# QK-norm attention with a max-out feed-forward layer: two-transfer row loads, fewer turning products, alternating spread products, idle products at the start, and first-layer bounds by one ones-product

## The chip, the core and the metric

The kernel runs on one core of a Trainium2 chip. The metric is the device time of one execution in microseconds (us), from the first instruction to the last with the little that lies around it. The time before is the median of three runs. One further execution was recorded by the hardware profiler; every duration below is from that execution.

The core has five engines, each with its own instruction stream that it works through in order: TensorE (PE in the profile; its weight loads are PEld) multiplies matrices into PSUM; VectorE (DVE), ScalarE (ACT) and GpSimd (POOL) work on elements; SyncE (SP) issues most of the DMA transfers, and ACT's stream issues some.

## The reference

```
def rmsnorm(x, g):
    rms = np.sqrt(np.mean(x * x, axis=-1, keepdims=True) + 1e-06)
    return x / rms * g
q_n, k_n = (rmsnorm(q, g_q), rmsnorm(k, g_k))
scores = np.matmul(q_n, k_n.transpose(0, 1, 3, 2)) / np.sqrt(64)
scores = scores - np.max(scores, axis=-1, keepdims=True)
attn = np.exp(scores)
attn = attn / (np.sum(attn, axis=-1, keepdims=True) + 1e-09)
x = np.matmul(attn, v)          # then heads side by side: 3584 x 768
h = np.maximum(np.maximum(x @ w1, x @ w2), x @ w3)
return (h @ w_out).astype(np.float32)
```

q, k and v are 8 batches of 12 heads of 448 tokens of 64 values; each of the four weight matrices is 768 x 768; everything is float32.

## The kernel before

Two heads make a pair; there are 48 pairs, g = 0 to 47. A pair's 896 rows of q (or k) lie as seven blocks of 128 rows: even blocks and the lower half of the last one hold the first head, odd blocks and its upper half the second. Of each pair, squares, row sums, an inverse root and a scaling normalise q and k (squares, sum_squares, inv_rms, scale_rows); the result is turned so that the 64 values lie across partitions; scores, softmax, and the product with v follow. A score tile is 128 queries of both heads against 448 keys; a pair has three such tiles and a fourth of 64 queries each.

The first six pairs (PLAIN = 6) work in plain float32: their rows are turned by TensorE (turn_whole writes the tile rows, keep_whole copies it to kt and qt), the exponentials are turned by TensorE (turn_plain, keep_turned), and the sums are inverted (inverse_sums), spread over the partitions by products with the identity (spread_sums) and applied at the end (scale_plain). Later pairs split every operand in two float16 parts and are turned by DMA.

The feed-forward layer multiplies with weights split in two float16 parts. load_raw brings a block of raw weights, prep_block decodes it (one step on ACT, three on DVE), and after three blocks of one row of output features bound_in finds a bound of that row's columns: 18 products of the block with itself (tile marks), the largest entry of each row on DVE, then the largest over the partitions, which the helper largest does by a turning product, a DVE reduction over one partition and a product with a row of ones. From the bound come a root on POOL, a copy, a reciprocal and a multiply on DVE (w_most, w_up), and the two-part split of the three blocks (upper on ACT, lower on DVE).

The order is written out by hand. Every engine runs its instructions in the order in which the program makes them. The main loop goes through 12 beats for each pair (beat(g, i)); in a beat stand pieces of pair g (softmax, scores), of g - 1 (values), of g + 1 (turning) and of g + 2 (squares), plus units of the feed-forward layer (thirds) from the seventh pair on. later(n, work) puts work n beats behind the present one; bound_in and prep_block use it, and one weight block is taken every four beats, so that six rows of features are prepared in six pairs and a little more.

Ahead of the loop stands the opening: loads of pairs 0 and 1 and of the first three raw blocks, normalisation of both pairs, the product of the two gains (the tile gain; column and gain_c carry it to partitions; prep_gain derives factors for later pairs), turning of pair 0, and the first score tile.

A ring of three PSUM buffers (tag "m") serves marks, rows, spread and the small tiles; score tiles have two buffers of their own.

## Time and profile before

| what | us |
|---|---|
| median of three runs (1033.67, 1035.94, 1036.47) | 1035.94 |
| the profiled execution, time | 1033.57 |
| its span, first to last instruction | 1031.8 |
| mean granted TensorE clock | 0.985 |
| TensorE busy, 0 to 10 us | 0.82 |
| TensorE busy, 300 to 400 us | 100.00 |

The table is read from its ends. The profile's busy times say how full an engine was, not whether it set the time: TensorE is 96% busy over the whole span, but nearly idle at first, full from 300 us on, and in between it shares the work with VectorE, which is fuller than TensorE in some stretches. A change in an early stretch has to be read from that stretch.

### The profile page before, as it was taken

How to read it: one execution, taken by the hardware profiler on the slowest of the kernel's cores; microseconds unless marked ns; L12 is line 12 of the kernel's file. 1: busy time of each engine (PE TensorE's matmuls, PEld its weight loads, DVE VectorE, ACT ScalarE, POOL GpSimd, SP SyncE). 2: the span in 40 equal slices, each digit the busy share in tenths (PEclk: the TensorE clock that was granted, in tenths of full speed). 3: DMA queues.
4: the chain of work that ended last, by engine and by line, in shares of the span. 5: the costliest groups of instructions: out<-in, count | busy, mean ns of one | idle time of the engine just before them, and what ended most of it. 6: DMA issues, size and time to landing. Idle time of an engine off the chain costs nothing.

```text
span 1031.8 us, 17413 instructions
## 1 busy us (share of the span) xinstructions
PE 988.9 (96%) x5988; PEld 530.6 (51%) x5988; DVE 697.5 (68%) x1343; ACT 622.8 (60%) x1419; POOL 598.5 (58%) x652
## 2 busy tenths in 40 slices
PE   5999789898899999999999999999999999999998
PEld 3655444444455555555555555555555555555555
DVE  4898989987676856776667767786777666760120
ACT  3787866667666676666665666666665766651111
POOL 5566676765766666756666576676675766410000
PEclk9999879999999999999999999999999999999999
DMA  8866698997999999999999899999999998861001
GB/s 200 202 178 172 165 204 164 177 166 134 209 173 171 167 182 210 168 172 151 221 171 188 152 216 181 177 169 180 193 168 169 179 201 145 135 104 59 1 1 62
DMA packets 524089, 165.99 MB, mean 161 GB/s; under 512 B 500321, under 2 KB 519777, under 8 KB 524001
## 3 DMA queue, kind: packets, MB, share of 16 engines
q1 hardware_dynamic: 460992, 148.89, 74.8%
q10 hardware_dynamic: 63008, 16.00, 8.7%
q8 instruction: 47, 0.77, 0.3%
q14 instruction: 42, 0.34, 0.1%
HBM read 53.35 MB, written 11.01 MB: 62 GB/s over the span
## 4 chain that ended last, share of the span: by engine, by line
PE 74%; DVE 2%; ACT 1%; DMA 1%; issue 1%; SPq 0%; ACTq 0%
PE acc L841 41%; PE acc L903 15%; PE av L812 8%; PE sc L633 8%; PE sc L640 1%; DVE pp L767 1%; DVE nm L655 1%; DMA pt<-pp 1%; ACT sc L671 0%; DVE w_sb L335 0%; DVE ss L413 0%; DMA out_dram<-osb 0%; SPq L786 0%; ACT w_sb L330 0%; ACT pp L757 0%
## 5 line engine op out<-in xcount | busy, mean ns | idle before, releaser
L841 PE MATMUL acc<-xt,w_sb 128*128 128x448 f16 x2592 | 516.8, 355 | 0.0
L841 PEld LDWEIGHTS <-w_sb 128*128 128x128 f16 x2592 | 252.5, 98 | 245.0 <-issue 16.8
L671 ACT ACTIVATE sc<-sc,nm 128x448 f32<-128x448 f32 x294 | 178.8, 608 | 197.0 <-DVE nm L655 192.5
L655 DVE TENSOR_REDUCE nm<-sc 128x2 f32<-128x896 f32 x192 | 186.3, 970 | 101.5 <-PE sc L640 51.4
L757 ACT ACTIVATE pp<-sc,rs 128x448 f16<-128x448 f32 x294 | 172.8, 633 | 77.9 <-issue 29.2
L767 DVE SCALAR_TENSOR_TENSOR pp<-sc,rs,pp 128x448 f16<-128x448 f32 x294 | 188.0, 675 | 3.3 <-ACT pp L757 3.2
L427 POOL TENSOR_TENSOR ri<-ri,half_neg 128x7 f32<-128x7 f32 x96 | 148.8, 1550 | 8.0
L903 PE MATMUL acc<-w_sb,ht 128*128 128x384 f16 x864 | 148.6, 327 | 0.0
L461 POOL TENSOR_TENSOR kp<-kn,kp 128x448 f16<-128x448 f32 x42 | 44.7, 1065 | 167.6 <-ACT kp L455 154.5
L633 PE MATMUL sc<-kt,qt 128*128 128x448 f16 x504 | 117.6, 356 | 10.4 <-DVE pp L767 7.7
L903 PEld LDWEIGHTS <-ht 128*128 128x128 f16 x864 | 83.8, 99 | 60.2 <-issue 5.8
L633 PEld LDWEIGHTS <-qt 128*128 128x128 f16 x504 | 48.8, 98 | 56.0 <-issue 6.9
L812 PE MATMUL av<-pt,vp 128*64 128x448 f16 x672 | 72.2, 355 | 0.7 <-DMA pt<-pp 0.6
L870 POOL COPY hx<-ht 128x128 f16<-128x128 f16 x48 | 15.3, 318 | 94.3 <-DVE ht L865 94.3
L413 DVE TENSOR_REDUCE ss<-sq 128x7 f32<-128x448 f32 x96 | 57.6, 601 | 11.4 <-ACT sq L404 8.3
L595 POOL TENSOR_TENSOR vp<-vr,vp 128x512 f16<-128x512 f32 x42 | 50.0, 1189 | 22.6 <-ACT vp L589 22.6
L750 DVE TENSOR_SCALAR rs<-sc 128x2 f32<-128x2 f32 (+1 forms) x168 | 26.2, 156 | 50.4 <-ACT sc L671 50.3
L827 DVE SCALAR_TENSOR_TENSOR xt<-av,xt 128x448 f16<-128x448 f32 x42 | 26.2, 623 | 49.0 <-ACT xt L826 49.0
L461 POOL TENSOR_TENSOR qp<-qn,qp 128x448 f16<-128x448 f32 x42 | 46.2, 1100 | 19.2 <-ACT qp L455 16.9
L855 DVE TENSOR_TENSOR m<-acc,m 128x448 f32<-128x448 f32 x48 | 29.6, 617 | 37.7 <-PE acc L841 37.5
L812 PEld LDWEIGHTS <-vp 128*64 128x64 f16 x672 | 35.0, 109 | 35.0 <-issue 15.5
L861 ACT ACTIVATE ht<-acc 128x448 f16<-128x448 f32 x48 | 26.2, 546 | 41.8 <-DVE acc L855 41.8
(130 smaller groups left out, 1181.4 us busy)
## 6 DMA issues: line engine op xcount, KB each, us to landing
raw<-in_moe_w_dram SPq DMA_DIRECT2D x18, 768.0 KB, 4.5
kt<-kt SPq DMA_DIRECT2D x84, 112.0 KB, 2.5
out_dram<-osb SPq DMA_DIRECT2D x24, 384.0 KB, 3.7
vr<-in_v_dram SPq DMA_DIRECT2D x42, 192.0 KB, 4.1
kr<-in_k_dram ACTq DMA_DIRECT2D x34, 224.0 KB, 3.3
qr<-in_q_dram ACTq DMA_DIRECT2D x34, 224.0 KB, 4.6
raw<-in_moe_w_out_dram SPq DMA_DIRECT2D x6, 768.0 KB, 5.0
vs<-vp SPq DMA_DIRECT2D x84, 48.0 KB, 2.1
```

Source lines behind the costliest of these rows:

```text
L413: nc.vector.tensor_reduce(sums[g % 2][:, KQ[what]], sq, axis=AX, op=ALU.add)
L427: nc.gpsimd.tensor_tensor(out=ri, in0=ri, in1=half_neg[:, at], op=ALU.pow)
L461: nc.gpsimd.tensor_tensor(out=parts[:, :, 1], in0=n, in1=parts[:, :, 0], op=ALU.subtract)
L595: nc.gpsimd.tensor_tensor(out=vp[:, 1], in0=values_of(g).rearrange("p h n d -> p (h n) d"), in1=vp[:, 0], op=ALU.subtract,)
L633: nc.tensor.matmul(sc[:, h, :S], qt[:, 4 * h + c], kt[:, n, keys[h]], start=n == 0, stop=n == 1,)
L655: nc.vector.tensor_reduce(nm[:, :n], sc[:, :n, :S], axis=AX, op=ALU.max, negate=True)
L671: nc.scalar.activation(to, sc[:, h, :S], AF.Exp, bias=nm[:, h:h + 1], accum_out=total,)
L757: nc.scalar.activation(pp[:, h, 0], sc[:, h, :S], AF.Copy, scale=rs[:, h:h + 1])
L767: nc.vector.scalar_tensor_tensor(out=pp[:, h, 1], in0=sc[:, h, :S], scalar=rs[:, h:h + 1], in1=pp[:, h, 0], op0=ALU.mult, op1=ALU.subtract,)
L812: nc.tensor.matmul(av[half, :S], values, pt[:, 7 * h + block, SHIFT[h]:SHIFT[h] + S], start=n == 0, stop=n == len(steps) - 1,)
L841: nc.tensor.matmul(acc[:, :S], wt[:, wp, c], xs[c][:, xp], start=(c == 0 and n == 0), stop=(c == NCT - 1 and n == 2),)
L903: nc.tensor.matmul(acc[:, :HW], lhs, wo_sb[:, f, wp, half * HW:(half + 1) * HW], start=(f == 0 and n == 0), stop=(f == NFT - 1 and n == 2),)
```

## The change

Seven edits, all in work that is done ahead of the later part of the span.

1. Row loads of the first six pairs take two transfers (four blocks and three blocks) in place of three. For pair 0 the second transfer of q goes to ACT's queue.
2. load_v brings the first batch's v in three transfers of four consecutive rows a partition, in place of four transfers of single rows; keep_whole writes kt in the matching order of keys.
3. turn_whole turns the last block by two 64 x 64 products on separate quarters of the array, in place of three products; kt and qt are 448 columns wide, in place of 512.
4. spread_sums goes through the column halves in alternation.
5. 36 products of the identity with itself, read as bfloat16, stand at the start of TensorE's stream; their result is not used.
6. In the opening the squares of pair 1 stand behind those of pair 0, the sums and roots of pair 1 move up, and prep_gain moves back.
7. bound_in takes one product of a full square of ones with the row maxima (their sum, in place of their maximum); the root becomes an inverse root with a multiply on POOL, and the splits come earlier by one to three beats. bound_out computes w_most by two operations once.

```
+    idle = ps_m.tile([P, 512], F32, name="idle", tag="m")
+    bits = ident.bitcast(BF16)
+    for _ in range(WARM):
+        nc.tensor.matmul(idle[:, :2 * P], bits[:, :P], bits, start=True, stop=True)
...
         def reduce():
             row_largest(most, box[0][:, 0:P])
-            largest(most, clear, (1, 1, 2, 1))
+        def spread():
+            box.append(ps_m.tile([P, 512], F32, name="most", tag="m"))
+            nc.tensor.matmul(
+                box[1][:, 0:1], ones_c.broadcast_to([P, P]), most, start=True, stop=True
+            )
...
-            nc.gpsimd.tensor_tensor(out=w_up[:, ft:ft + 1], in0=most, in1=root, op=ALU.pow)
-            later(2, scale)
+            up = w_up[:, ft:ft + 1]
+            nc.gpsimd.tensor_tensor(out=up, in0=most, in1=half_neg[:, 0:1], op=ALU.pow)
+            nc.gpsimd.tensor_scalar(
+                out=up, in0=up, scalar1=2.0 * UP, scalar2=1.0, op0=ALU.mult, op1=ALU.mult
+            )
+            later(3, scale)
         def scale():
-            top, up = w_most[:, ft:ft + 1], w_up[:, ft:ft + 1]
-            nc.vector.tensor_copy(top, up)
-            nc.vector.reciprocal(up, top)
-            nc.vector.tensor_scalar(
-                out=up, in0=up, scalar1=2.0 * UP, scalar2=None, op0=ALU.mult
-            )
+            up = w_up[:, ft:ft + 1]
...
-                later(2 + 4 * j, lambda n=n, f=f: upper(n, f), True)
-                later(4 + 4 * j, lambda n=n, f=f: lower(n, f), True)
-        later(2, products)
-        later(4, reduce)
+                later(4 * j, lambda n=n, f=f: upper(n, f), True)
+                later(2 + 4 * j, lambda n=n, f=f: lower(n, f), True)
+        for at, work in ((2, products), (4, reduce), (5, spread), (7, clear)):
+            later(at, work)
...
     def bound_out():
+        nc.vector.reciprocal(w_most, w_up)
+        nc.vector.tensor_scalar(
+            out=w_most, in0=w_most, scalar1=2.0 * UP, scalar2=None, op0=ALU.mult
+        )
...
-            for h in range(2):
-                on[h].dma_start(out=t[:, h:6:2], in_=rows[:, 4 * h:4 * h + 3])
-            on[1].dma_start(out=t[:, 6], in_=rows[:, 3])
+            on[0].dma_start(out=t[:, 0:7:2], in_=rows[:, 0:4])
+            on[1].dma_start(out=t[:, 1:6:2], in_=rows[:, 4:7])
...
-            for u in range(4):
+            wrap = KEYS - LEFT // 4
+            for h, to, of in (
+                (0, slice(0, KEYS), slice(0, S)),
+                (1, slice(0, wrap), slice(LEFT, S)),
+                (1, slice(wrap, KEYS), slice(0, LEFT)),
+            ):
                 nc.sync.dma_start(
-                    out=vr[:KEYS, :, u],
-                    in_=rows[:, u * KEYS:(u + 1) * KEYS].rearrange("h p d -> p h d"),
+                    out=vr[to, h::2].rearrange("p h u d -> p h (u d)"),
+                    in_=rows[h::2, of].rearrange("h (p u) d -> p h (u d)", u=4),
                 )
...
-        for to, of, rows in (
-            (slice(0, LEFT), last, upper),
-            (slice(LEFT + 3 * P, 512), last, lower),
-            (slice(LEFT + 3 * P, 512), n[:, 6], lower),
-        ):
+        for half in HALVES:
             nc.tensor.matmul(
-                turned[:of.shape[1], to], of, ident[:, rows],
-                start=True, stop=True,
+                turned[half, 3 * P:S], n[half, 6], ident[half, half], start=True, stop=True
             )
...
-            nc.scalar.copy(t, turned)
+            nc.scalar.copy(
+                t.rearrange("p (u n) -> p n u", u=4),
+                turned[:, :S].rearrange("p (n u) -> p n u", u=4),
+            )
...
-        for h, half in enumerate(HALVES):
-            for c in range(3):
+        for c in range(3):
+            for h, half in enumerate(HALVES):
                 first = LEFT * h + c * P
                 nc.tensor.matmul(
                     spread[half, first:first + P],
...
+    for g in range(2):
+        for what in "kq":
+            squares(g, what)
     for what in "kq":
-        squares(0, what)
-    sum_squares(0, "k")
-    inv_rms(0, "k")
-    sum_squares(0, "q")
-    inv_rms(0, "q")
+        sum_squares(0, what)
+        inv_rms(0, what)
     nc.vector.tensor_tensor(out=gain, in0=gains[:, 0], in1=gains[:, 1], op=ALU.mult)
+    sum_squares(1, "k")
     scale_rows(0, "k")
+    sum_squares(1, "q")
     scale_rows(0, "q")
+    turn_whole(0, "k")
...
-    prep_gain()
-    for what in "kq":
-        turn_whole(0, what)
+    turn_whole(0, "q")
     for what in "kq":
         keep_whole(0, what)
-    for what in "kq":
-        squares(1, what)
-        sum_squares(1, what)
         inv_rms(1, what)
+    prep_gain()
```

The first place is VectorE's stream in the opening; ss_88 holds the sums of pair 0 before (ss_125 after), ss_89 those of pair 1 (ss_126 after). Before:

```order
L413 TENSOR_REDUCE ss_88<-sq 128x7 x2
L1016 TENSOR_TENSOR gain<-gains 128x64
L435 TENSOR_TENSOR kn<-kr,ri 128x448
L435 TENSOR_TENSOR qn<-qr,ri 128x448
L172 TENSOR_REDUCE g_top<-gain 128x1
L985 TENSOR_SCALAR g_top<-g_top 128x1
```

and now:

```order
L440 TENSOR_REDUCE ss_125<-sq 128x7 x2
L1035 TENSOR_TENSOR gain<-gains 128x64
L440 TENSOR_REDUCE ss_126<-sq 128x7
L462 TENSOR_TENSOR kn<-kr,ri 128x448
L440 TENSOR_REDUCE ss_126<-sq 128x7
L462 TENSOR_TENSOR qn<-qr,ri 128x448
L180 TENSOR_REDUCE g_top<-gain 128x1
```

Pair 1's two sums have moved from behind the whole of prep_gain to places ahead of pair 0's kn and qn.

The second place is POOL's stream in the opening, from the second root of pair 0 on. Before:

```order
L427 TENSOR_TENSOR ri<-ri,half_neg 128x7
L1005 TENSOR_TENSOR even<-even,root 128x1
L423 TENSOR_SCALAR ri<-ss_89 128x7
L427 TENSOR_TENSOR ri<-ri,half_neg 128x7
L423 TENSOR_SCALAR ri<-ss_89 128x7
L427 TENSOR_TENSOR ri<-ri,half_neg 128x7
L435 TENSOR_TENSOR kn<-kr,ri 128x448
```

and now:

```order
L454 TENSOR_TENSOR ri<-ri,half_neg 128x7
L450 TENSOR_SCALAR ri<-ss_126 128x7
L454 TENSOR_TENSOR ri<-ri,half_neg 128x7
L450 TENSOR_SCALAR ri<-ss_126 128x7
L454 TENSOR_TENSOR ri<-ri,half_neg 128x7
L1024 TENSOR_TENSOR even<-even,root 128x1
L462 TENSOR_TENSOR kn<-kr,ri 128x448
```

The root of the gain (even) has moved behind the two roots of pair 1, so that these follow those of pair 0 directly.

The third place is TensorE's stream in the second pair, where the bound of the first row of features is found. Before:

```order
L691 MATMUL turned<-ident,e 112x128 x8
L157 MATMUL marks<-ident,most 1x128
L624 MATMUL sc<-kt,qt 128x448 x2
L691 MATMUL turned<-ident,e 112x128 x8
L164 MATMUL most<-top,ones 128x1
L624 MATMUL sc<-kt,qt 128x448 x2
L691 MATMUL turned<-ident,e 112x128 x4
L490 MATMUL rows<-ident,kn 128x128 x3
L501 MATMUL rows<-ident,kn 128x64 x2
L501 MATMUL rows<-ident,kn 64x64
```

and now:

```order
L709 MATMUL turned<-ident,e 112x128 x8
L285 MATMUL most<-most,ones_c 128x1
L643 MATMUL sc<-kt,qt 128x448 x2
L709 MATMUL turned<-ident,e 112x128 x8
L643 MATMUL sc<-kt,qt 128x448 x2
L709 MATMUL turned<-ident,e 112x128 x4
L517 MATMUL rows<-ident,kn 128x128 x3
L522 MATMUL rows<-ident,kn 64x64 x2
```

One product of the bound is left, at the place of the first, and two small products finish the turning where three stood.

More of the change, by code (lines that the diff above doesn't have):

```diff
@@ L42 @@
 LOADS = 14
+WARM = 36
 @with_exitstack
@@ L364, in load_q @@
     def load_q(g):
-        load_rows(g, "qr", q, (nc.sync, nc.sync) if g < LOADS else (nc.scalar,))
+        first = (nc.sync, nc.sync if g else nc.scalar)
+        load_rows(g, "qr", q, first if g < LOADS else (nc.scalar,))
     def load_k(g):
@@ L490, in turn_whole @@
             nc.tensor.transpose(
-                turned[:, LEFT + c * P:LEFT + (c + 1) * P],
+                turned[:, c * P:(c + 1) * P],
                 n[:, 2 * c:2 * c + 2].rearrange("p h d -> p (h d)"), ident,
             )
-        last = n[:, 5:7].rearrange("p n d -> p (n d)")
-        lower, upper = HALVES
-        for to, of, rows in (
-            (slice(0, LEFT), last, upper),
-            (slice(LEFT + 3 * P, 512), last, lower),
-            (slice(LEFT + 3 * P, 512), n[:, 6], lower),
-        ):
+        for half in HALVES:
             nc.tensor.matmul(
-                turned[:of.shape[1], to], of, ident[:, rows],
-                start=True, stop=True,
+                turned[half, 3 * P:S], n[half, 6], ident[half, half], start=True, stop=True
             )
@@ L511, in keep_whole @@
             t = sb.tile([P, 2, UNITS * P], F16, name="kt", bufs=2)
[L512 to L513 removed]
+            t = t.rearrange("p a n -> p (a n)").bitcast(F32)[:, :S]
+            nc.scalar.copy(
+                t.rearrange("p (u n) -> p n u", u=4),
+                turned[:, :S].rearrange("p (n u) -> p n u", u=4),
+            )
         else:
             t = sb.tile([P, 8, P], F16, name="qt", bufs=2)
[L516 to L517 removed]
+            t = t.rearrange("p n r -> p (n r)").bitcast(F32)[:, :S]
+            nc.scalar.activation(t, turned[:, :S], AF.Copy, scale=gain_c)
         s[what + "s"] = t
@@ L618, in scores @@
             for h, rows in enumerate(HALVES):
-                if c < 3:
-                    to, cols = sc[:, h, :S], slice(LEFT + c * P, LEFT + (c + 1) * P)
-                else:
-                    to = sc[rows, 0, :S]
-                    cols = slice(0, LEFT) if h else slice(LEFT + 3 * P, 512)
+                to = sc[:, h, :S] if c < 3 else sc[rows, 0, :S]
                 nc.tensor.matmul(
-                    to, qt[rows, cols], kt[rows, SHIFT[h]:SHIFT[h] + S],
-                    start=True, stop=True,
+                    to, qt[rows, c * P:min((c + 1) * P, S)], kt[rows], start=True, stop=True
                 )
@@ L731, in spread_sums @@
                 )
+        for h, half in enumerate(HALVES):
             first = 0 if h else 3 * P
```

7 lines of the change are left out of this document (2 added, 5 removed).

## The prediction

> **What bounds the kernel now.** I read the page's totals first, then busy time by stretches, then busy time by pair of heads, then the timeline of the stretches in which TensorE is not full. In the rows by stretch the columns are: the stretch and its length, then busy us (and instructions) of PE, PEld, DVE, ACT and POOL, the granted clock, the DMA share and GB/s.
>
> ```profile
> PE 988.9 (96%) x5988; PEld 530.6 (51%) x5988; DVE 697.5 (68%) x1343; ACT 622.8 (60%) x1419; POOL 598.5 (58%) x652
> ...
> 0.00:10.00 10.00, 0.82 (x6) 0.74 (x7) 2.12 (x9) 2.81 (x5) 3.39 (x10) 1.00 0.55 130
> 10.00:20.00 10.00, 7.02 (x26) 4.23 (x24) 5.34 (x14) 4.31 (x9) 5.55 (x7) 1.00 1.20 300
> ...
> 300.00:400.00 100.00, 100.00 (x616) 53.41 (x616) 70.96 (x140) 65.23 (x153) 67.67 (x78) 1.00 1.01 181
> ```
>
> From 300 us on PE is full and the change touches nothing there (the order of PE's instructions is the same behind the last first-layer block). So the end moves only if the work of the first 300 us is done earlier: what is saved there, on whichever engine is late, moves everything behind it by as much, since the order is fixed and nothing waits for a clock. In the first 20 us no engine is full: this is one chain of waits. Then come the six pairs in plain float32 (g = 0 to 5), where two engines share the bound. The next rows cut the span at the row maxima and rescalings of successive pairs.
>
> ```profile
> 23.00:46.30 23.30, 23.30 (x181) 14.79 (x178) 18.90 (x32) 17.34 (x42) 17.33 (x16) 1.00 0.93 230
> 46.30:63.20 16.90, 16.43 (x118) 10.06 (x117) 14.91 (x27) 13.62 (x31) 10.94 (x9) 1.00 0.52 152
> 63.20:81.70 18.50, 16.63 (x118) 10.06 (x117) 17.38 (x28) 15.06 (x33) 10.21 (x9) 1.00 0.47 134
> 81.70:102.40 20.70, 19.46 (x133) 11.80 (x131) 18.26 (x30) 15.38 (x34) 13.21 (x12) 0.92 0.75 206
> 102.40:120.90 18.50, 15.68 (x98) 8.72 (x97) 17.56 (x28) 14.69 (x33) 13.22 (x11) 0.91 0.65 154
> 120.90:142.50 21.60, 14.77 (x91) 7.87 (x89) 21.20 (x42) 15.43 (x34) 15.98 (x14) 0.79 0.77 181
> ```
>
> PE is full in the first stretch; from the second on DVE is the fuller engine, with 2.0, 1.1, 2.4, 0.9 and 0.4 us idle. Both halves of the change (fewer PE products, fewer DVE steps) therefore act where their engine counts.
>
> **Term 1, the opening.** The rows are start, duration, engine, line, operation, and in brackets the idle time before it with what ended it; the last one is a row of DMA issues (count, KB, us to landing), for the q transfer that was issued at 2.29.
>
> ```profile
> 2.29 0.49 SPq L359 DMA_DIRECT2D qr<-in_q_dram  x1
> 7.60 0.58 ACT L404 ACTIVATE sq<-qr 128x448 f32<-128x448 f32 x1 [2.54 <-DMA kr<-in_k_dram]
> 8.92 0.64 POOL L423 TENSOR_SCALAR ri<-ss 128x7 f32<-128x7 f32 x1 [1.32 <-DVE ss L413]
> 9.55 0.90 PE L490 MATMUL rows<-ident,kn 128*128 128x128 f32 x3 [0.16 <-DVE kn L435]
> 9.64 1.50 POOL L427 TENSOR_TENSOR ri<-ri,half_neg 128x7 f32<-128x7 f32 x1
> 11.17 0.62 DVE L435 TENSOR_TENSOR qn<-qr,ri 128x448 f32<-128x448 f32 x1 [1.68 <-POOL ri L427]
> 14.74 3.36 PE L624 MATMUL sc<-kt,qt 64*128 64x448 f32 x8 [0.84 <-ACT qt L517]
> 15.89 0.21 POOL L423 TENSOR_SCALAR ri<-ss 128x7 f32<-128x7 f32 x1 [2.70 <-DVE ss L413]
> 19.02 0.87 ACT L192 ACTIVATE raw<-raw 128x768 f32<-128x768 f32 x1
> 19.50 0.93 POOL L435 TENSOR_TENSOR kn<-kr,ri 128x448 f32<-128x448 f32 x1
> 22.58 0.58 ACT L513 COPY kt<-rows 128x512 f32<-128x512 f32 x1 [2.69 <-PE rows L501]
> 23.06 0.64 ACT L671 ACTIVATE e<-sc,nm 128x448 f32<-128x448 f32 x1
> 25.20 0.49 PE L490 MATMUL rows<-ident,qn 128*128 128x128 f32 x3
> ...
> qr<-in_q_dram SPq DMA_DIRECT2D x1, 32.0 KB, 5.2
> ```
>
> There are two chains to the second exponential at 23.06. The first: the last piece of q lands at 2.29 + 5.2 = 7.5, its square starts at 7.60, POOL's inverse root (0.64 + 1.50) lets qn start at 11.17, the scores start at 14.74, and the raw block's rescaling on ACT ends at 19.89. The second: pair 1's squares stand behind pair 0's qt on ACT, so POOL starts on pair 1's roots only at 15.89 and its kn is done at 20.43; kt then waits for the turned rows until 22.58. The second chain is the later one by 2.69 us, the idle time of the 22.58 row.
>
> After the change pair 1's squares stand on ACT behind pair 0's, ahead of gain_c. POOL does four roots one after another, of 0.21 + 1.50 each: if q lands with k the fourth ends near 12.7, with the gain's root in front (one column; counted at 0.6, well below the 1.50 of seven) kn of pair 1 is done at 14.2 instead of 20.43; if q lands as late as now it is done at 16.1. So the second chain moves up by 4.3 to 6.2 us, and the first becomes the late one. In it, DVE must first do the sum of pair 1's k and then of its q ahead of kn and qn, 0.62 each; SP issues three transfers fewer up to pair 1's k and four up to its q, 0.49 each, which should bring them 1.5 to 2 us earlier. I take qn at 9.9, that is 1.3 earlier (bounds: 0 where pair 1's q lands as now, 2.0). The array is slow here: the same three transposes take 0.90 at 9.55 and 0.49 at 25.20. Fewer products and a fast array take about 0.9 off the two turnings, and 0.66 off the first two score products. From the scores' start to the end of the rescaling is 19.89 - 14.74 = 5.15. So scores start at 14.74 - 1.3 - 0.9 = 12.5, the rescaling ends at 17.0, the second exponential starts at 17.5: **5.5 us earlier** (3.3 with q as late as now and a slow array, 6.5 at best).
>
> The clock column reads 1.00 in both stretches, so here only the durations show the slow array. The Trainium skill ("TensorE: Matmul & The Clock Gate", Part 1) says that the array starts at half clock, gets the full one after some 3.4 us of sustained work, and falls back after an idle window as long. Part 4 of the same page says that transposes do not count as work for this. The trace agrees with the slow start, and rather with Part 4 than with the 3.4 us: 7.02 us of PE work between 10 and 20 us, much of it transposes, did not end it. By Part 1 the 36 idle products warm the array, it stays so, and the sum stands; by Part 4, with little but transposes between 9 and 13 us, it may be slow again at the scores, and the sum would be 1.5 us smaller.
>
> The 36 idle products cost PE time that is empty now (0.82 busy in the first 10 us). A 128-column bf16 product takes 0.07 us fast (the 40.68 row below, 1.21 for 18), so 256 columns take 0.13 to 0.23, and 36 take 4.7 to 8.3. They start when the identity is written, in the second microsecond, and end between 6 and 10 us: hidden, or at worst some tenths late.
>
> **Term 2, PE's products in pairs 0 to 5.**
>
> ```profile
> 36.39 3.23 PE L801 MATMUL av<-pt,vr 112*64 112x448 f32 x16
> 39.94 0.81 PE L501 MATMUL rows<-ident,qn 128*128 128x64 f32 x6
> 40.68 1.21 PE L265 MATMUL marks<-w_sb 128*128 128x128 bf16 x18
> 41.82 0.87 PE L727 MATMUL spread<-ident,sum 128*64 128x128 f32 x6
> 43.93 0.86 PE L543 MATMUL marks<-vr 128*128 128x128 bf16 x12
> 46.64 0.38 PE L157 MATMUL marks<-ident,most 128*1 128x128 f32 x2
> 48.92 0.38 PE L164 MATMUL most<-top,ones 1*128 1x1 f32 x2
> ```
>
> The three last turning products take 40.68 - 39.94 = 0.74; two on separate quarters of the array take 0.25 to 0.5: 0.45 less, twice a pair. The spread takes 43.93 - 41.82 = 2.11 for eight products in one column half after the other. The values product, which alternates halves, does 16 passes of 448 columns in 3.23, 0.45 ns a column, against 0.87/6/128 = 1.13 ns here; at that rate the spread's 16 passes (1792 columns) take 0.8. I take 1.0 less (bounds 0 and 1.3). The two products of the bound, 0.38 each with their ends lying over the next product, become one: 0.3 less. Together 2.2 us a pair. This counts where something waits for PE; on DVE that is:
>
> ```profile
> 41.93 0.29 DVE L172 TENSOR_REDUCE most<-marks 128x1 f32<-128x128 f32 x1 [0.82 <-PE marks L265]
> 44.83 0.29 DVE L172 TENSOR_REDUCE v_rows<-marks 128x1 f32<-128x128 f32 x1 [2.61 <-PE marks L543]
> 62.63 0.63 DVE L655 TENSOR_REDUCE nm<-sc 128x1 f32<-128x448 f32 x1 [1.67 <-PE sc L624]
> 81.19 0.62 DVE L655 TENSOR_REDUCE nm<-sc 128x1 f32<-128x448 f32 x1 [0.77 <-PE sc L624]
> 100.68 0.29 DVE L172 TENSOR_REDUCE v_rows<-marks 128x1 f32<-128x128 f32 x1 [2.14 <-PE marks L543]
> 120.40 0.62 DVE L655 TENSOR_REDUCE nm<-sc 128x1 f32<-128x448 f32 x1 [0.75 <-PE sc L624]
> ```
>
> Each wait shrinks by what PE saves ahead of it and by no more than itself: 1.9 of the first two, 1.67, 0.77, 1.45 (one turning and the spread) and 0.75, together 6.5. PE itself waits for ACT between these places, so I take three quarters: **5.0 us** (0 to 8.8, the sum of the rows).
>
> **Term 3, DVE's steps of the first-layer bounds.**
>
> ```profile
> 52.23 0.15 DVE L283 COPY w_most<-w_up 128x1 f32<-128x1 f32 x1
> 52.68 1.24 DVE L209 SCALAR_TENSOR_TENSOR w_sb<-raw,w_sb 128x768 uint32<-128x768 uint32 x1
> 63.96 0.28 DVE L160 TENSOR_REDUCE top<-marks 1x1 f32<-1x128 f32 x1 [0.16 <-PE marks L157]
> ```
>
> Gone from each of six blocks: 52.68 - 52.23 = 0.45 for three small steps, and the 0.28 of the 63.96 row, 0.21 without the end that lies over the next step, with its 0.16 of wait at three of them: 6 x 0.66 + 0.5 = 4.4. Two small steps come back once in the second-layer bound, about 0.4, and the sixth block lies where DVE has slack: **3.7 us** (2.5 to 4.4). POOL's extra multiply per block (0.2, like the 15.89 row) lies in POOL's idle time, which is 5 us or more per pair in the table above; bare it would cost 1.2. The splits of the weights come three beats earlier, with nothing waiting for them.
>
> **At nothing:** the kt copy with its scattered write (448 instead of 512 elements, 0.58 now; ACT has 3 us idle per pair; 3.6 over six pairs if it took twice as long), the three transfers per v tile instead of four, which PE's v products do not wait for now, and the summed bound, which changes scales only.
>
> **The sum:** 5.5 + 5.0 + 3.7 = 14.2. The profiled execution took 1033.57 us (1031.8 of span and 1.8 around it): 1019.4. That execution lies below the three runs (median 1035.94); the same saving from the median gives 1021.7. I forecast 1020.5, between the two.
>
> **Rivals.**
> *Smaller, 1024 to 1029 (0.25).* Only part arrives: pair 1's rows land late and stand, through their sums, ahead of qn on DVE (term 1 at 3.3), or the array is slow again at the scores (1.5 less), or the waits for PE turn into waits for ACT (term 2 at 2). 3.3 + 2 + 3.7 = 9, 5 if both sink lower. For it: PE already waits for ACT ahead of scores in each pair.
> *Larger, 1010 to 1016 (0.14).* All waits for PE go. The cap: DVE's idle time in the six stretches is 4.4 + 6.8 = 11.2, with term 3 and 6.5 of opening 21.4, so 1012 to 1014. ACT, with 15 of 18.5 busy, caps a pair at about 3.4.
> *Nothing to be measured (0.06), within 0.3% or 3.1 us, about what a measurement of this kernel can tell from no change.* The idle products warm nothing, q lands as now and the pairs run at ACT's and DVE's pace: 3.3 with a loss on kt's copy of 2 or 3.
> *Slower, 1037 to 1042 (0.03).* A PE with less work rests more in the pairs and is granted less clock. The clock column reads 1.00 in the three fullest stretches and 0.92, 0.91 and 0.79 in the others, which is 1.7 + 1.7 + 4.5 = 7.9 us of clock lost. At 0.79 in all six (119.5 us in all) it would be 25, that is 17 more, and the 14.2 would be gone if no other engine covered it; from 0.76 on it would be slower by over 0.3%. Against it: DVE is busy through those stretches now and hides most of what PE loses.
>
> My forecast (1016 to 1024) has 0.52. The range of 8 in 10 reaches into both neighbours: 1012 to 1029. Faster by over 0.3%: 0.52 + 0.25 + 0.14 = 0.91; the same 0.06; slower 0.03.
>
> **What would show it.** Term 1: the second exponential (now 23.06) at 17 to 18, kn of pair 1 off POOL by 15, the first three transposes at 0.5. Term 2: the spread's 2.11 near 1.0, and the bracketed waits for PE gone or under 0.7. Term 3: stretches of pairs 1 to 4 shorter by 1.5 to 2 each. I would be wrong if pair 1's sums hold up qn, if the stretches keep their length with DVE waiting for ACT, or if PE has new idle time between 160 and 300 us.

## The result and the profile after

The changed kernel took 1029.13 us (median of six runs, 1027.15 to 1032.62), the kernel before 1035.91 on the same chip: a ratio of 0.9938 (95% interval 0.9920 to 0.9955), 6.8 us less. It is faster, by half of the 14.2 us that I had summed up, and 0.1 us beyond the slow end of my range. The execution that was profiled is the slowest of its six (1032.62, span 1030.4); the same kernel measured a second time (again) gave 1029.92, and its profiled execution 1028.51 (span 1026.4).

The totals of the changed kernel, as its page gives them:

```profile
PE 986.5 (96%) x5988; PEld 525.8 (51%) x5988; DVE 697.3 (68%) x1321; ACT 624.1 (61%) x1419; POOL 596.9 (58%) x658
```

PE's busy time is 2.4 us lower than before although the idle products add 6.5 to it, and DVE's stayed, with 22 instructions fewer. The busy time by stretch follows, with the columns of the prediction; the granted clock is the share of its full rate that the profile shows for TensorE. The stretches of 15 to 23 us are pairs 1 to 5:

```profile
0.00:10.00 10.00, 6.47 (x36) 4.65 (x36) 1.45 (x7) 2.64 (x4) 4.11 (x10) 1.00 0.56 144
10.00:20.00 10.00, 6.68 (x31) 3.43 (x33) 6.38 (x16) 3.94 (x9) 6.99 (x9) 0.66 0.98 282
...
46.00:61.60 15.60, 14.61 (x118) 8.66 (x116) 15.50 (x24) 14.90 (x34) 8.96 (x8) 1.00 0.53 144
61.60:82.30 20.70, 17.36 (x114) 9.46 (x114) 19.06 (x24) 15.75 (x36) 14.28 (x13) 0.84 0.62 181
82.30:103.20 20.90, 18.26 (x126) 10.20 (x122) 17.19 (x26) 15.21 (x35) 12.78 (x11) 0.84 0.62 159
103.20:121.10 17.90, 14.56 (x92) 7.54 (x89) 17.56 (x24) 14.14 (x32) 13.37 (x11) 0.81 0.74 169
121.10:143.20 22.10, 14.95 (x94) 8.71 (x92) 21.40 (x37) 15.54 (x34) 15.66 (x16) 0.84 0.72 178
...
300.00:400.00 100.00, 100.00 (x623) 53.35 (x621) 69.86 (x140) 65.43 (x153) 67.90 (x77) 1.00 0.99 183
```

Pair 1 is shorter than before (15.6 against 16.9), but pairs 2 and 3 are longer (20.7 and 20.9 against 18.5 and 20.7), and their granted clock is 0.84 where it was 1.00 and 0.92. The work that was taken away came back as slower work. From 300 us on PE is full, as before.

Next the changed kernel's opening, rows of its timeline in order of time across the engines (start, duration, engine, line, operation, and in brackets the idle time before it with what ended it).

```profile
1.35 6.47 PE L152 MATMUL idle<-ident 128*128 128x256 bf16 x36 [1.35 <-POOL ident masks.py:199]
10.57 0.22 DVE L1035 TENSOR_TENSOR gain<-gains 128x64 f32<-128x64 f32 x1 [4.31 <-DMA gains<-in_g_k_dram]
10.71 0.58 ACT L431 ACTIVATE sq<-kr 128x448 f32<-128x448 f32 x1 [5.09 <-DMA kr<-in_k_dram]
12.52 0.55 PE L517 MATMUL rows<-ident,kn 128*128 128x128 f32 x3 [4.70 <-DVE kn L462]
12.91 0.61 DVE L462 TENSOR_TENSOR qn<-qr,ri 128x448 f32<-128x448 f32 x1
13.69 0.90 PE L517 MATMUL rows<-ident,qn 128*128 128x128 f32 x3
15.79 3.36 PE L643 MATMUL sc<-kt,qt 64*128 64x448 f32 x8 [0.80 <-ACT qt L540]
16.52 0.92 DVE L1025 TENSOR_SCALAR gain<-gain,even 128x64 f32<-128x64 f32 x1 [1.69 <-POOL even L1024]
18.83 0.63 ACT L689 ACTIVATE e<-sc,nm 128x448 f32<-128x448 f32 x1 [3.09 <-DVE nm L673]
21.59 0.66 ACT L689 ACTIVATE e<-sc,nm 128x448 f32<-128x448 f32 x1
```

The second exponential moved from 23.06 to 21.59, not to 17.5. DVE came to the gain's product 2.5 us sooner than before and then waited 4.31 us for the gains; ACT waited 5.09 us for pair 1's rows, whose sums now stand ahead of kn and qn on DVE. So qn is 1.74 later than before, not 1.3 earlier. The idle products end at 7.82; after an empty stretch of 4.70 us the first transposes are still fast (0.55), the next ones, at 13.69, slow (0.90), and so are the scores (3.36, as before). Then prep_gain's last step waits 1.69 us for POOL's root, ahead of the first row maximum.

And the place where pair 2 loses its time, from the same timeline, with rows of DVE, POOL, ACT and PE.

```profile
62.11 1.60 DVE L212 SCALAR_TENSOR_TENSOR w_sb<-raw,w_sb 128x768 uint32<-128x768 uint32 x1
62.86 1.65 POOL L462 TENSOR_TENSOR qn<-qr,ri 128x448 f32<-128x448 f32 x1
63.74 1.58 DVE L217 SCALAR_TENSOR_TENSOR w_sb<-raw,w_sb 128x768 uint32<-128x768 uint32 x1
65.98 0.33 PE L522 MATMUL rows<-ident,kn 64*64 64x64 f32 x4
67.88 0.64 ACT L689 ACTIVATE e<-sc,nm 128x448 f32<-128x448 f32 x1 [2.01 <-DVE nm L673]
69.27 1.86 PE L643 MATMUL sc<-kt,qt 64*128 64x448 f32 x4 [2.96 <-ACT e L689]
71.06 1.96 PE L709 MATMUL turned<-ident,e 128*112 128x128 f32 x8
72.95 3.98 PE L820 MATMUL av<-pt,vr 112*64 112x448 f32 x16
...
78.74 0.87 PE L745 MATMUL spread<-ident,sum 128*64 128x128 f32 x12
79.54 0.33 PE L752 MATMUL spread<-ident,sum 64*64 64x64 f32 x4
```

The sizes of the edits came out: two products end the turning in 0.33 (0.27 up to the next group, in another place of the same trace, where it was 0.74), and the spread takes about 1.0 (78.74 to 79.71, where the next product starts) instead of 2.11. But PE is now through with the turning while DVE is still decoding weights; ACT waits 2.01 for DVE's row maximum and PE 2.96 for ACT. In the kernel before, the same score product waits 0.80:

```profile
70.16 1.02 PE L624 MATMUL sc<-kt,qt 64*128 64x448 f32 x4 [0.80 <-ACT e L671]
```

After the longer wait PE is slow: 1.86, 1.96 and 3.98 against 1.02, 1.09 and 3.23 for the same three groups before the change, 2.5 us lost behind one wait.

### The profile page after: what moved, and what is told of

It is laid out like the page before. It is cut to its first block, busy times and chain, and to the rows that moved or that the text cites. A ratio compares the mean times of both kernels' runs of the same rounds, so it can differ in the third digit from the quotient of the medians.

```text
span 1030.4 us, 17384 instructions
## 1 busy us (share of the span) xinstructions
PE 986.5 (96%) x5988; PEld 525.8 (51%) x5988; DVE 697.3 (68%) x1321; ACT 624.1 (61%) x1419; POOL 596.9 (58%) x658
## 4 chain that ended last, share of the span: by engine, by line
PE 76%; DVE 4%; ACT 1%; issue 1%; DMA 1%; SPq 0%; ACTq 0%; DVEq 0%
PE acc L860 42%; PE acc L922 15%; PE sc L651 8%; PE av L831 8%; PE sc L658 1%; DVE pp L786 1%; DVE nm L673 1%; DMA pt<-pp 1%; ACT sc L689 0%; DVE w_sb L354 0%; DVE ss L440 0%; ACT pp L776 0%; DMA out_dram<-osb 0%; DVE w_sb L208 0%; DVE w_sb L217 0%
## 5 line engine op out<-in xcount | busy, mean ns | idle before, releaser
L454 POOL TENSOR_TENSOR ri<-ri,half_neg 128x7 f32<-128x7 f32 x96 | 146.1, 1522 | 8.0
L846 DVE SCALAR_TENSOR_TENSOR xt<-av,xt 128x448 f16<-128x448 f32 x42 | 26.1, 622 | 47.7 <-ACT xt L845 47.7
L450 POOL TENSOR_SCALAR ri<-ss 128x7 f32<-128x7 f32 x54 | 17.5, 325 | 61.7 <-DVE ss L440 60.9
L831 PEld LDWEIGHTS <-vp 128*64 128x64 f16 x672 | 35.0, 109 | 34.8 <-issue 14.2
```

The source lines that it names most:

```text
L454: nc.gpsimd.tensor_tensor(out=ri, in0=ri, in1=half_neg[:, at], op=ALU.pow)
L831: nc.tensor.matmul(av[half, :S], values, pt[:, 7 * h + block, SHIFT[h]:SHIFT[h] + S], start=n == 0, stop=n == len(steps) - 1,)
```

## The experiments

Every median stands beside runs of the kernel before on the same chip (1034.4 to 1035.5). For the kernels that the argument turns on, this table cuts one profiled execution of each at the start of DVE's rescaling of pair 0 and of pair 5 (av<-av,by in the timeline of DVE): the opening with pair 0, the five pairs between, and the rest of the span.

| kernel | to pair 0's rescaling | pairs 1 to 5 | rest | span |
|---|---|---|---|---|
| before | 46.3 | 96.2 | 889.3 | 1031.8 |
| the change, first execution | 46.0 | 97.2 | 887.2 | 1030.4 |
| again (the change) | 43.0 | 96.7 | 886.7 | 1026.4 |
| opening_only | 46.2 | 96.2 | 890.4 | 1032.8 |
| pe_only | 44.3 | 93.8 | 888.7 | 1026.8 |
| bound_only | 47.7 | 97.9 | 885.3 | 1030.9 |
| pe_bound | 44.1 | 96.6 | 888.1 | 1028.8 |
| keepwarm | 44.3 | 93.9 | 888.9 | 1027.0 |
| best | 40.9 | 93.3 | 885.3 | 1019.5 |
| best_again | 42.0 | 93.3 | 888.6 | 1023.9 |
| best_nowarm | 40.1 | 96.4 | 886.3 | 1022.8 |
| best_oldbound | 41.7 | 94.2 | 888.8 | 1024.7 |
| before_warm | 48.4 | 97.3 | 888.4 | 1034.1 |

The middle column repeats within 0.5 us (97.2 and 96.7 for the change, 93.3 twice for best); the other two can differ by 1 to 3 us between executions of one kernel.

### The opening: what holds the rows up

**again** is the changed kernel itself.

> The changed kernel once more, for a second trace and a tighter time. Every theory expects 1027 to 1031 us. If the half-clock stretches of TensorE decide how much of the pairs' saving is lost, an execution with a higher mean granted clock than the 0.975 of the first trace should be shorter, by some 3 to 5 us at 0.98, and its pairs 2 to 5 shorter in the stretches that then read 1.00; if VectorE and GpSimd slow each other, pairs 2 to 5 last 20.7, 20.9, 17.9 and 22.1 us again whatever the clock.

1029.92 (ratio 0.9950, interval 0.9936 to 0.9964), second exponential at 20.41. **gains_one** changes only the gains' load, to one partition (the others hold ones):

```
-            out=gains[:, i], in_=src.rearrange("(o d) -> o d", o=1).broadcast_to([P, D])
+            out=gains[0:1, i], in_=src.rearrange("(o d) -> o d", o=1)
```

> The changed kernel with the two gains brought to one partition only (256 bytes each) instead of to all 128; the other partitions hold ones, so pairs from the seventh on get a wrong gain. Theory A (the two transfers that read one row 128 times hold up all that is queued with them): the hole in the DMA rate between 5 and 7.5 us goes, pair 1's k lands before 8 us instead of 10.6, the second exponential starts near 17 to 18 instead of 21.6, and the time falls by 2 to 4 us. Rival B (the hole comes from something else, as the order or number of transfers on SP's queue): the hole stays, pair 1's k lands at 10 or later, and the time is the changed kernel's within 1 us.

1027.87 (0.9925, 0.9911 to 0.9938). First the DMA issues of the changed kernel's first 12 us (count, KB, us to landing):

```profile
kr<-in_k_dram SPq DMA_DIRECT2D x1, 96.0 KB, 8.3
gains<-in_g_q_dram ACTq DMA_DIRECT2D x1, 32.0 KB, 8.1
```

Two stretches of its busy time, whose last two columns are the DMA share and GB/s, and the same two of gains_one:

```profile
5.00:6.00 1.00, 1.00 (x6) 0.71 (x5) 0.35 (x1) 0.58 (x1) 0.92 (x2) 1.00 0.26 59
6.00:7.00 1.00, 1.00 (x10) 0.84 (x8) 0.27 (x1) 0.00 (x0) 0.91 (x2) 1.00 0.16 38
```
```profile
5.00:6.00 1.00, 1.00 (x11) 0.89 (x10) 0.29 (x2) 0.58 (x1) 0.71 (x2) 1.00 1.06 191
6.00:7.00 1.00, 1.00 (x12) 0.85 (x9) 0.77 (x3) 0.75 (x2) 1.00 (x1) 1.00 0.82 176
```

And two rows of DVE's timeline in gains_one:

```profile
6.36 0.22 DVE L1034 TENSOR_TENSOR gain<-gains 128x64 f32<-128x64 f32 x1
14.02 0.92 DVE L1024 TENSOR_SCALAR gain<-gain,even 128x64 f32<-128x64 f32 x1 [2.74 <-POOL even L1023]
```

Two transfers that read one row of 256 bytes 128 times hold up what is queued with them: the rate falls to 59 and 38 GB/s, the gains land after 8.1 us and the 96 KB of pair 1's k after 8.3. With one read each the hole is gone, the gain is there at 6.36 instead of 10.57, pair 1's k is squared at 6.20 instead of 10.71, and the second exponential starts at 18.73. What is late next is prep_gain's last step, now 2.74 us behind POOL's root. **even_late** is gains_one with that step moved to the twelfth beat:

```
-        nc.vector.tensor_scalar(
-            out=gain, in0=gain, scalar1=even, scalar2=None, op0=ALU.mult
-        )
+        later(12, even_gain)
```

> The changed kernel with the gains loaded to one partition (as in the run gains_one: later pairs' gain is then wrong) and the last step of the gain's preparation, which waits for POOL's power, moved from the opening to the twelfth beat. Theory A (this step holds DVE up ahead of the first row maximum: 2.74 us of wait in gains_one): the first exponential at 13 to 14 (15.97 in gains_one), the second at 16 to 17 (18.73), and 1.5 to 2.5 us below gains_one, 1025.5 to 1026.5. Theory B (the time is taken back in pairs 2 and 3, as most of the opening's gain was): the exponentials as in A, the median within 0.7 us of gains_one's 1027.87.

The second exponential came to 16.81 and pair 0's rescaling to 39.5 (41.3 in gains_one); the median, 1028.85 (0.9934, 0.9914 to 0.9954), shows no gain over gains_one, though its profiled execution was its fastest (1025.66). Whether the 1.8 us reach the end is not settled by these medians. **no_idle** is the changed kernel without the 36 idle products.

> The changed kernel without the 36 idle products. Theory A (they warm the array only until about 13 us, and it is slow again before the scores): only the three first transposes slow down, 0.55 to 0.90, and the time is the changed kernel's within 1 us. Rival B (the early warmth reaches into the first pair): second exponential over 1 us later and the time 1 to 3 us longer.

1028.35 (0.9934, 0.9916 to 0.9952): they bring nothing that can be measured. **opening_only** is the kernel before with edits 1, 5 and 6, and **before_gains** the kernel before with the gains' load of gains_one.

> The kernel before with only the opening of the change: idle products, first rows in two transfers, the new order of the norms and turnings. Theory A (the opening gives what the changed kernel's second exponential shows, 23.06 to about 20.4 to 21.6): the second exponential at 20.5 to 22, and 1.5 to 2.5 us faster than the kernel before, 1033 to 1034. Theory B (what the opening gains is waited away by the first plain pair's end, as the gain of 0.3 at the end of pair 1 in the first trace of the changed kernel suggests): the second exponential as in A, but the time within 1 us of the kernel before.

> The kernel before with the gains loaded to one partition, the others set to one (later pairs' gain is then wrong), and nothing of the change. Theory A (the 128-fold reads of one row hold the queues up whatever stands beside them: the rows of pair 0's q land behind them, sq of q at 7.60): the hole in the DMA rate at 4 to 6 us is gone, the square of q at 5.5 to 6.5, the second exponential at 21 to 22 instead of 23.06, and 1 to 2 us faster, 1033 to 1034. Theory B (in the old order q's rows are late by their place in the queue): q's square within 0.5 of 7.6 and the time within 0.7 us.

opening_only: 1034.41 (0.9984, 0.9973 to 0.9995), second exponential at 23.27. Alone, the opening's part does not bring the second exponential forward, and the first comes 3.0 us later (20.78 instead of 17.78): its gains too land at 10.4, and pair 1's k at 10.6. before_gains: 1034.16 (0.9984, 0.9974 to 0.9994); q's square moved from 7.60 to 4.95 and the second exponential to 21.52, but pair 0's rescaling only from 46.3 to 46.0. So the hole was there before the change (44 GB/s from 4 to 6 us, where before_gains has 170 and 125). Most of the 1.5 us won is lost again in pair 0: its first turning products of the exponentials take 1.92 us instead of 1.09, and a score tile waits 0.42 for ACT where it did not wait.

### The parts apart

**pe_only** is the kernel before with edits 3 and 4 (and the copy of kt contiguous); **bound_only** the kernel before with edit 7; **pe_bound** both.

> The kernel before with only TensorE's part of the change: turning in three transposes and two 64x64 products, the alternating spread, the narrower copies of keys and queries (the second head's keys then meet other values). The opening's order, its DMAs and the bounds are as before. Theory A (my prediction's term 2: what TensorE saves is waited for): 4 to 5 us faster than the kernel before, about 1031. Theory B (TensorE's saving turns into waits for ACT's exponentials, behind which it runs at half clock): turning 0.25 to 0.3, spread 1.0 to 1.1, the clock's column falls below 1.00 in pair 2, and the time is within 1.5 us of the kernel before, 1034 to 1036.

> The kernel before with only the change of the first-layer bounds: spread by one ones-product, clear, power of minus one half and a product on POOL, the three DVE steps gone and the reciprocals at the end. Theory A (my prediction's term 3: DVE is the busiest engine of the pairs and its steps are on the path): 3 to 4 us faster, about 1032. Theory B (DVE's steps lie in its waits, or DVE is slowed by POOL's longer work): within 1 us of the kernel before.

> TensorE's part and the bounds' part of the change together, on the opening and the DMAs of the kernel before (contiguous copy of the keys). TensorE's part alone gave 5.7 us, the bounds' part alone 1.2, the opening's part alone 1.1, and the changed kernel only about 6. Theory A (the parts add, and the opening of the change takes back what it gives): 1028 to 1029, 6.5 to 7.5 below the kernel before. Theory B (once TensorE's work is shorter, DVE and POOL overlap and slow each other, so the bounds' part adds nothing or takes away): 1029.5 to 1031, at or above the 1029.9 of TensorE's part alone; pair 2 then takes 19 to 21 us instead of 18.4.

pe_only: 1029.86 (0.9939, 0.9924 to 0.9953), 5.7 us. bound_only: 1034.30 (0.9987, 0.9973 to 1.0001), 1.2 us, with an interval that includes no change. pe_bound: 1030.32 (0.9946, 0.9928 to 0.9963): the bounds add nothing to PE's part. Pair 2 in the busy time by stretch, pe_only first, then pe_bound:

```profile
59.52:77.92 18.40, 16.42 (x114) 9.06 (x113) 17.92 (x29) 15.03 (x33) 11.11 (x10) 0.91 0.54 154
```
```profile
59.70:80.46 20.76, 17.43 (x113) 9.57 (x114) 18.80 (x24) 15.29 (x35) 13.96 (x13) 0.84 0.63 182
```

And the score product of pair 2 that waits, from PE's timeline, in the same order:

```profile
66.82 1.76 PE L613 MATMUL sc<-kt,qt 64*128 64x448 f32 x4 [1.54 <-ACT e L659]
```
```profile
67.39 1.87 PE L624 MATMUL sc<-kt,qt 64*128 64x448 f32 x4 [2.95 <-ACT e L670]
```

With the bounds' part PE waits 2.95 instead of 1.54, and pair 2 is 2.4 us longer though DVE has five instructions fewer. In the table edit 7 costs 1.7 us in pairs 1 to 5 by itself and 2.8 on top of edits 3 and 4; it gives time back behind them. From the start of xt on ACT for pair 5 to its start for pair 6, the fourteen profiled executions with edit 7 take 24.5 to 25.9 us, the six without it 26.8 to 28.7 (28.4 before, 24.5 in bound_only, 24.7 in the change). The rows of the sixth bound say why, the kernel before first, then bound_only:

```profile
141.50 0.59 PE L157 MATMUL marks<-ident,most 128*1 128x128 f32 x2 [2.74 <-DVE most L172]
142.91 6.19 PE L841 MATMUL acc<-xt,w_sb 128*128 128x448 f16 x21
149.44 0.16 DVE L274 TENSOR_SCALAR most<-most 128x1 f32<-128x1 f32 x1 [2.44 <-PE most L164]
```
```profile
143.74 0.38 PE L277 MATMUL most<-most,ones_c 128*128 128x1 f32 x2 [1.61 <-DVE most L172]
144.55 4.15 PE L852 MATMUL acc<-xt,w_sb 128*128 128x448 f16 x21
148.21 0.15 DVE L282 TENSOR_SCALAR most<-most 128x1 f32<-128x1 f32 x1
```

Before the change the bound's second product stands behind 21 feed-forward products (acc), and DVE waits for it, 2.44 us here and 1.3 to 2.8 in the six executions. Now the only product stands ahead of them, and DVE does not wait.

**kt_plain** writes kt contiguously in the changed kernel, **kt_oldv** has the old loads of v as well.

> The changed kernel with the copy of the turned keys written contiguously, as it was before the change (which key meets which value then differs in the plain pairs, so the output does too; the number and size of all operations is the same). Theory A (the scattered write costs what its rows say, 0.92 to 0.96 against 0.58, and ACT is what the pairs wait for): the copy comes back to 0.55 to 0.6, and of 0.35 us in each of six plain pairs most is gained, 1 to 2 us, median 1028 to 1029 beside the changed kernel's 1029.9. Theory B (the pairs are set by TensorE at the lower clock and by DVE beside POOL; ACT's copy lies in slack): the copy is shorter, the time is the same within 0.5 us.

> The changed kernel with the contiguous copy of the keys and the value rows loaded as before the change, in four transfers per tile (keys and values then agree as they did before). Theory A (the three wider transfers land later, and TensorE's waits of 1.25 and 1.21 us for the value rows in pair 1 are on the path): no such waits, pair 1 shorter by 1 to 2 us, median 1028 to 1029 beside 1029.75 with the new loads. Theory B (ACT or DVE is late there anyway): the waits are gone or shorter, the time within 0.5 us of 1029.75.

1029.75 (0.9942, 0.9923 to 0.9961) and 1030.88 (0.9964, 0.9948 to 0.9979). The scattered copy costs ACT 0.92 instead of 0.53, and the end nothing that can be measured; nor do the new loads of v.

### The clock behind the waits

**keepwarm** puts products of the identity, into a PSUM tile that the next turning overwrites, ahead of the score tile that waits:

```
                 if early:
+                    if i == 3 and 0 < g < PLAIN:
+                        stir(8 if g == 1 else 16)
                     scores(*divmod(k + 1, 4))
```

> The changed kernel with 16 more idle products (8 in pair 1) ahead of the one score tile per pair, in pairs 1 to 5, before which TensorE waits 1 to 3 us for the exponentials. Theory A (the saving of the pairs is lost because TensorE rests there and is then granted half the clock for the next 4 to 6 us): the clock reads 1.00 through most of pairs 2 to 5, the score products there take 1.02 instead of 1.86, and the time falls by 4 to 8 us. Rival B (the saving is lost to VectorE and GpSimd slowing each other): the clock rises too, but pairs 2 to 5 keep their length and the time is the changed kernel's within 1.5 us. Rival C (the products stand in the way): the time grows by up to 2 us a pair.

1026.80 (0.9920, 0.9902 to 0.9937), 3 us below the changed kernel, and 93.9 us instead of 96.7 in pairs 1 to 5. **before_warm** is the kernel before with the same.

> The kernel before with the identity products of keepwarm (8 in the first, then 16 ahead of the score tile that waits in pairs 2 to 6) and nothing of the change. Theory A (the half clock behind waits of 2 to 3 us is a loss of TensorE's own, and in the kernel before it costs little, since its clock column shows 1.00 in pair 2 and falls to 0.92 only in pair 3): 1033.5 to 1035, with pair 3 shorter than 20.6 by 1. Theory B (identity products help whatever the kernel, by the 3 us seen on the changed one): 1031.5 to 1032.5.

1035.91 (1.0005, 0.9997 to 1.0014): nothing. The length of a wait alone does not decide what follows it: in pair 3 of pe_only 1.67 us were followed by full speed (1.02, 1.09, 3.23), in pair 3 of the kernel before 0.80 by slow products (1.55, 1.95). Then **best**: the changed kernel with keepwarm's products, the late step of even_late, and gains loaded to one partition and spread by

```
+    wide = ps_m.tile([P, 512], F32, name="wide", tag="m")
+    nc.tensor.matmul(wide[:, 0:D], ones, gain[0:1], start=True, stop=True)
```

> A kernel that computes what the reference asks for: the changed kernel with the gains loaded to one partition and spread by a ones-product, the last step of the gain's preparation at the twelfth beat, and identity products ahead of the score tile that waits in pairs 2 to 6 (8 in the first, then 16). Theory A (the three effects add: gains 2, late step 2, clock 3): 1023 to 1024.5. Theory B (the opening's gain is taken back by DVE and POOL in the pairs): 1025.5 to 1027, about what the identity products alone gave (1026.8).

1023.06 (0.9883, 0.9865 to 0.9901). To see what carries it, best once more and **best_nowarm**, without the products in the pairs:

> The run named best once more, unchanged, so that the next run has it beside it on one chip. Every theory expects what it gave before, 1022 to 1024.5; it tells how far two calls lie apart, on which the reading of best_oldbound (1026.32) and best_steps (1026.69) rests.

> The run named best without the identity products in pairs 2 to 6 (those of the opening stay). Theory A (the half clock behind ACT's waits is what the changed kernel loses in pairs 2 and 3): clock 0.84 to 0.91 there, pair 2 of 19 to 21 us and pair 3 of 20 to 21.5 instead of 17.2 and 19.5, and 3 to 5 us slower than best, 1026.5 to 1028. Theory B (the identity products change something else, and the two mends of the opening carry the gain): within 1 us of best.

best_again: 1025.82 (0.9914, 0.9901 to 0.9928); best_nowarm: 1028.09 (0.9938, 0.9924 to 0.9951). Pairs 2 and 3 in the busy time by stretch, best_again first, then best_nowarm:

```profile
57.86:75.03 17.17, 16.24 (x128) 9.65 (x127) 16.82 (x25) 15.22 (x33) 10.35 (x10) 1.00 0.56 158
75.03:94.57 19.54, 18.61 (x149) 11.18 (x147) 18.70 (x26) 16.66 (x36) 14.91 (x13) 1.00 0.83 219
```
```profile
55.65:74.91 19.26, 15.91 (x112) 8.99 (x112) 18.51 (x24) 15.15 (x34) 13.65 (x13) 0.91 0.57 172
74.91:96.08 21.17, 18.27 (x125) 10.28 (x126) 16.89 (x25) 15.39 (x35) 13.10 (x12) 0.84 0.68 177
```

And around pair 2's waiting score product, from PE's timeline, in the same order:

```profile
63.06 1.92 PE L704 MATMUL turned<-ident 128*128 128x256 bf16 x16
65.54 1.02 PE L643 MATMUL sc<-kt,qt 64*128 64x448 f32 x4 [0.56 <-ACT e L689]
```
```profile
63.34 1.08 PE L643 MATMUL sc<-kt,qt 64*128 64x448 f32 x4 [2.98 <-ACT e L689]
64.35 1.96 PE L720 MATMUL turned<-ident,e 128*112 128x128 f32 x8
66.24 3.87 PE L831 MATMUL av<-pt,vr 112*64 112x448 f32 x16
```

With the products the clock stays at 1.00 and the two pairs take 36.7 us instead of 40.4. In pair 2 the three groups behind the wait take 6.9 us without them and 5.3 with them, which is 1.6 of the 2.1 us between the two. That filling the waits is worth some 4 us in these two pairs is shown, and that in pair 2 most of it is PE's slower products; at the end it is 2.3 against best_again and 5.0 against best.

**best_oldbound** undoes edit 7 in best, **best_steps** adds only three column steps on DVE for each bound, into a tile that nothing reads. There are six bounds in the traces, not the 13 to 16 that the two expectations reckon with.

> The run named best with the bounds' part of the change undone: the old spread of the largest by a row maximum, the square root on POOL, and three DVE steps for each of the sixteen bounds. Theory A (the bounds' part is worth what my prediction gave it, 3.7 us, once the clock is held and TensorE is no longer late): 1026 to 1027, against 1023.06. Theory B (the steps lie where DVE is not waited for, or the longer work on POOL and the other order cost what they save): 1022.5 to 1024.

> The run named best with a copy, a reciprocal and a multiplication of one column on DVE added at each bound, into a tile that nothing reads: the three steps that the change took away, and nothing else of the old bounds. Theory A (DVE's column steps are on the path, 0.46 us in each of the bounds; three quarters of 13 to 16 bounds reach the end): 4 to 6 us slower, or at least 2, 1025 to 1028. Theory B (they lie in slack, or change only how DVE and POOL fall beside each other): within 1 us of best, 1022.5 to 1024.

1026.32 (0.9916, 0.9899 to 0.9933) and 1026.69 (0.9915, 0.9898 to 0.9932). Against best that reads 3.3 and 3.6, as my term 3 had it; against best_again 0.5 and 0.9. The nine runs of best and best_again together have a median of 1024.82: 1.5 and 1.9, with intervals that overlap. With the waits filled, edit 7 shortens pairs 1 to 5 by 0.9 (94.2 to 93.3), where without that it lengthens them by 2.8, and the stretch from xt of pair 5 to xt of pair 6 by 4.1 (28.7 to 24.6); the three steps alone cost 1.2 and 0.5 there. But best and best_again, the same kernel, differ by 3.3 in the rest, nearly all of it later than that stretch. So the worth of edit 7 at the end stays open between nothing and 3.6.

## Why the prediction was twice too large

I summed up 14.2 us, and 6.8 came. At the second exponential the two executions of the changed kernel are 1.5 and 2.7 us ahead instead of 5.5. From there to pair 5's rescaling they take 2.2 more and 0.2 less than the kernel before, where terms 2 and 3 had promised 8.7 less. The last 2.1 and 2.6 come behind pair 5.

**Term 2, PE's products (5.0): the size came by luck.** pe_only gives 5.7, but 1.9 of it are there at the second exponential (21.16 instead of 23.06): mostly the shorter turnings of the opening, which I had counted in term 1. From there to pair 5's rescaling it gives 2.5, half of the term. The six waits for PE that I listed did shrink as I said, from 8.8 us to 2.7; two of them in pe_only, at 1.67 and 2.14 before:

```profile
58.98 0.62 DVE L643 TENSOR_REDUCE nm<-sc 128x1 f32<-128x448 f32 x1 [0.26 <-PE sc L613]
95.46 0.29 DVE L172 TENSOR_REDUCE v_rows<-marks 128x1 f32<-128x128 f32 x1 [0.21 <-PE marks L536]
```

What failed is the share that I let arrive, three quarters. In pair 2 of pe_only PE waits 1.54 us for ACT instead of 0.80 and the product behind it takes 1.76, and that pair is only 0.2 us shorter. I had also read DVE as the fuller engine from the second stretch on; the rows show PE fuller in the second and the fourth (16.43 against 14.91, 19.46 against 18.26).

**Term 1, the opening (5.5): the step that failed most.** I let pair 1's rows come 1.5 to 2 us earlier because SP issues fewer transfers, and counted the gains as there. The opening's edits alone give 1.1. Pair 1's k was issued 1.7 us earlier (2.32 instead of 3.97), but it landed after 8.3 us, held up by the two 128-fold reads, as gains_one shows. The gain's product stood ahead of kn before as well; there DVE came to it at 8.74, behind q's late rows, when the gains had landed (7.9). Now DVE is ready at 6.3, and the gains land at 10.5 (9.1 in again); why they land later than before was not tried apart. Pair 1's sums are new ahead of kn and qn. I had named rows that land late, through their sums ahead of qn, as the rival "smaller"; the cause, and the wait for the gains ahead of kn, I had not seen, although the row of the gains' landing stood in the trace of before. I also moved prep_gain back without counting that its last step waits for POOL ahead of the first row maximum: 1.69 in the changed kernel, 2.74 in gains_one.

**Idle products: no gain.** They ended at 7.82, inside 6 to 10 as bounded, but the turned rows came at 12.52 and the scores were slow, the case of term 1 that is 1.5 us smaller. The Trainium skill ("TensorE: Matmul & The Clock Gate", Part 4) says that transposes do not count as work for the clock; the trace agrees: in gains_one little but transposes stood between the last idle product at 7.2 and the scores at 11.69, and these took 3.26. Where the scores began 3.2 to 3.4 us after the last idle product they took 1.77 (best, best_nowarm, best_steps), where 4.2 to 5.0 us after it 2.73 to 3.26 (even_late, best_again, gains_one, best_oldbound). Part 1 says that the window in which activity is counted runs freely, so that the same kernel may meet it at another phase; the traces fit this: the first transposes were fast (0.55) after an empty stretch of 4.70 us in the changed kernel and slow (0.90) after one of 3.89 us in kt_plain.

**Term 3, DVE's bound steps (3.7): cancelled, not absent.** The steps are gone, and the stretch from xt of pair 5 to xt of pair 6 shows the gain (3.9 in bound_only): at the sixth block, which I had put down to slack, and by a wait for PE that I had not listed. In pairs 1 to 5 the edit turned into a loss: PE waits longer for DVE and ACT, is granted a lower clock, and in pair 2 of the changed kernel takes 2.5 us more for the next 5.3 us of work. This is the mechanism of my rival "slower" (a PE with less work rests more and is granted less clock), for which I gave 0.03 on the ground that DVE covers what PE loses. It does not cover it: behind the slow products of pair 2 DVE itself waits for PE, 1.53 us at 78.85, where it had no wait before. The loss is smaller than the gain, so the sign stayed. (By that rival's own sum the kernel is slower by over 0.3% from a clock of 0.78 on, not 0.76.)

**At nothing: right in what I named.** The scattered copy and v's loads changed nothing measurable. POOL's power with an exponent of minus one half takes 1.26 instead of 0.80, which I had not counted; DVE's decoding steps take 1.58 to 1.60 instead of 0.96 where POOL works beside them, as in the rows of pair 2 above. The Trainium skill ("Trainium Architecture — The Big Picture", What this means for kernel authors) says that these two engines share a port by an exclusive lock; the trace agrees in kind, by 0.6 us a step. How much of edit 7's loss is this and how much the clock was not tried apart; filling the waits (keepwarm) takes 2.8 us off pairs 1 to 5, as much as edit 7 had added to them.

**The sum.** By the medians of the parts, 1.1 + 5.7 + 1.2 = 8.0, against 6.8 and 5.5 measured for the whole change. I had also let whatever is saved early reach the end whole; best and best_again show that the same code behind pair 5 can take 3.3 us more in one execution than in another.

## What to carry to other kernels

Work that is taken from an engine in a chain is won only up to the next engine's wait; where TensorE then waits, look at what its next products take, and fill the wait if the products can be had for nothing. Before an order is changed, look up when each operand lands now: an operand that arrived in somebody's shadow is a wait as soon as what stood ahead of its reader is done sooner. A part that measures as nothing may be a gain and a loss of equal size, and only the parts apart, and a run with the loss mended, tell this from an edit that does nothing.

## What I had not expected of the hardware

- Two transfers of 32 KB that read one 256-byte row for each of 128 partitions land after 8.1 and 7.9 us (5.0 and 6.5 in again) and take the queues' rate from over 130 down to 38 GB/s; with 0.2 KB each instead, it is 176 in the same microsecond of gains_one, though 68 in that of best.
- After 4.70 us without work PE's first transposes were still fast (0.55), and those 1.2 us later slow (0.90); after 3.89 us in kt_plain the first were slow at once.
- A wait of 2.96 us inside a pair costs 2.5 us more behind it; in again the same wait (2.97) was followed by a fast first product (1.02).
